# Retention attention and a two-layer MLP on one core: the first layer's weights move from GpSimd's casting DMAs into the token queue as fp32, with a cast on ScalarE

## The chip, the cores and the metric

The kernel runs on one core of a Trainium2 chip. The metric is the device time of one execution in microseconds, as the median of several runs; lower is better. In the rows of the profile PE is TensorE's matmuls, PEld its weight loads, DVE is VectorE, ACT is ScalarE, POOL is GpSimd and SP is SyncE, which here only issues DMAs.

## The reference, cut to what matters

```python
# q, k, v: fp32 [B=8, H=8, S=576, D=64]; w_in: fp32 [512, 2048]; w_out: fp32 [2048, 512]
scores = (q @ k.T) / sqrt(64)                     # per batch and head
gamma  = 1 - 2 ** (-5 - head)
Dmat   = where(i >= j, gamma ** (i - j), 0)       # causal decay
ret    = (scores * Dmat) @ v
x      = ret.transpose(0, 2, 1, 3).reshape(4608, 512)   # 4608 tokens
h      = x @ w_in                                 # first layer
g      = h * cos(h)
out    = g @ w_out                                # second layer, fp32 [4608, 512]
```

## The kernel before

**Attention.** Each sequence of 576 tokens is worked on in chunks of 64 with a running state. The kernel goes through *sessions*: the first eight take 128 tokens each (the methods `big_s` and `big`), the later ones two chunks of 64 from two streams. A session needs a tile of k and one of v (128 tokens by 512 columns, 256 KB as fp32) and a part of a tile of q (256 tokens, 512 KB), numbered in the order of use: k0, v0, q0 and so on, a new q for every second of the first sessions. SP loads them as fp32 into staging buffers: five slots `stg` for k and v, three `qstg` for q. ACT, DVE or POOL cast them to bf16 (`cast_k`, `cast_q`, `cast_v`; q and v are multiplied with decay weights as they are cast). TensorE transposes k and q (`step_tk`, `step_tq`) into PSUM, and DVE or ACT copy the result to `kt` and `qt` (`turn`). Then come the scores (`big_s`, L603), the mask by DVE (`pt`, L608), and one group of matmuls for the old state, the new state and the output (`big`, L624 to L633). The output goes to `xt`, the state to `sbd` (L584). From session 14 on the transposes are DMAs.

**First layer.** `mlp1` works on units of one PSUM bank: 512 columns, as 256 tokens by two blocks of 128 hidden features, 512 tokens by one, or 128 tokens by four. TensorE makes the unit (L711), ACT takes the cosine as a sine with a bias of pi/2 (L719), DVE multiplies (L722) into `gt`, of which there are two buffers, for even and for odd blocks of 512 tokens. There are six PSUM banks for all of this, one of them kept for filler matmuls at first. A unit needs the weights `win` of its features: `w_in` is cut into eight parts of 256 columns, w0 to w7, each for two blocks of features.

**Second layer.** For the first block of tokens `mlp2` (L736) multiplies directly; for the others `strassen` and `product` (L828) use sums of weights (`tw`, from `weight_sums`) and of tokens (`s5`, `s1`, from `token_sums`). ACT or DVE empty the banks to `os`, and SP stores.

**Order.** `schedule` adds all operations in a written order, with the pairs that may be mixed passed to `run`. A planner (`Prog.arrange`) then plays them through with assumed costs and, within a small window on each engine, takes the first that is ready in its own reckoning; in gaps of the first 24 us on TensorE it puts filler matmuls (L695). What comes out is a fixed order for each engine, with semaphore waits. Each engine works strictly in that order, and so does the queue of DMAs that SP issues.

**Weights.** `load_win` and `load_wout` are issued by POOL and cast in the DMA: fp32 in HBM, bf16 in SBUF. The five loads of `w_in` and the order with the tokens are set by these lines:

```python
WI = ((0, 1, 0), (1, 1, 0), (2, 2, 0), (4, 2, 2), (6, 2, 3))     # first part, parts, gate
GT = 1
load_to(need[0])                                                 # tokens of sessions 0 to 3
for x, n, t in WI:
    self.load_win(x, n, [("stg", t, 1, 0)] if t >= 0 else [])    # gate: v of slot t has landed
load_to(G1 + need[0], [("win", GT)])                             # next four sessions: wait for w1
```

The four loads of `w_out` (512 rows each) wait for the v tile in slot 0 (v5 at that time), and the tokens after k7 and v7 wait for the first part of `w_out`.

Of the kernel before, what the change touches and what calls it, by code (L numbers as in the profile page):

```python
# [8 lines left out]
F32 = mybir.dt.float32  # L9
# [3 lines left out]
DM, DFF = H * D, 2048  # L13
# [5 lines left out]
TB = 512  # L19
NTB = TOK // TB  # L20
NB = 6
AT = (9, 11, 12, 15)
GT = 1
C1 = ('pool', ('dve', 'pool'), 'pool')
EO, ES, EQ = ('dve', 'dve'), ('act', 'dve'), ('dve', 'dve')
WI = ((0, 1, 0), (1, 1, 0), (2, 2, 0), (4, 2, 2), (6, 2, 3))
G1, G2, WG = 4, 5, ("stg", 0, 1, 0)
FILL, SLOW = 24.0, 5.6
NF = DFF // 128
HF, HB = NF // 2, TB // 2  # L30
# [206 lines left out]
SOLO = 8  # L237


def sessions():  # L240
    out = [((uv, n), (uv, n + 1)) for uv in range(2) for n in range(0, SOLO, 2)] + [((0, SOLO),)]
    return out + [((0, n), (1, n - 1)) for n in range(SOLO + 1, NC)] + [((1, NC - 1),)]


SES = sessions()
NS = len(SES)

# [13 lines left out]
def place(uv, n):  # L261
    return SOLO * 64 * uv + 64 * n if n < SOLO else 256 * (n // 2) + 128 * uv + 64 * (n % 2)
# [14 lines left out]
def new_in(g, of):  # L277
    was = {of(*x)[0] for y in SES[:g] for x in y}
    return [x for x in dict.fromkeys(of(*x)[0] for x in SES[g]) if x not in was]


def ap(t, size, p0, n, off, *dims):
    return bass.AP(t, p0 * size + off, [[size, n]] + [list(d) for d in dims])


class Kernel:
    def __init__(self, nc, es, q, k, v, w_in, w_out, out):
# [17 lines left out]
        self.SBD = [sb(f"sbd{i}", [128, 1024], BF16) for i in range(self.NSB)]  # L305
        self.GT = [sb(f"gt{i}", [128, NF * TB], BF16) for i in range(2)]
        self.S5 = sb("s5", [128, HF * TB], BF16)
# [104 lines left out]
                bass.AP(self.src[0], (at // S * H * S + at % S) * D, [[2 * D, n], [S * D, H], [1, 2 * D]])),  # L412
                r=list(gate), w=[("qstg", slot, p0)], sem=f"q{slot}_{p0}", cost=0.62, ring=0.2 + 1.7 * n / 128, pkt=0.03)

    def load_win(self, s, n, gate=()):
        self.P.add("pool", lambda e: e.dma_start(
            ap(self.WIN, 4 * DFF, 0, 128, s * 256, [DFF, 4], [1, n * 256]),
            bass.AP(self.w_in, s * 256, [[DFF, 128], [128 * DFF, 4], [1, n * 256]])),
            r=list(gate), w=[("win", x) for x in range(s, s + n)], sem=f"wi{s}", cost=0.78, ring=1.35 * n, pkt=0.04 * n)

    def load_wout(self, s, gate=()):
        self.P.add("pool", lambda e: e.dma_start(
# [276 lines left out]
    def mlp1(self, lo, hi, fs):  # L699
# [3 lines left out]
        self.n_cb += 1  # L703
        cb, gt = self.CB[ci], self.GT[j % 2]
        xts = self.slots(lo, hi)
# [22 lines left out]
    def mlp2(self, j, t, fs, cols=(0, DM)):  # L728
        if fs[0] == 0:
            self.m2 = Box()  # L730
        box = self.m2
        gt, c0, cn = self.GT[j % 2], cols[0], cols[1] - cols[0]

# [47 lines left out]
    def token_sums(self, j, u):  # L781
        gt, f = self.GT[j % 2], 2 * u

# [19 lines left out]
    def product(self, j, m, box, t, at, first=True):  # L803
        gt = (self.GT[j % 2], NF * TB)
        wo, tw = (self.WOUT, NF * DM, DM), (self.TW, 3 * HF * HB, HB)
# [127 lines left out]
    def schedule(self):  # L933
        def req(x):
            return 1 + max(g for g in range(NS) if min(place(*y) for y in SES[g]) < x)

        need = [req(TB * (j + 1)) for j in range(NTB)]
        tiles, quads = ([new_in(g, of) for g in range(NS)] for of in (tile_of, quad_of))
        BYPE, LEAD = 14, 2
        at = {"load": 0, "cast": 0}  # L940

        def load_to(g, gate=()):
            while at["load"] < min(g, NS):
                x = at["load"]
                for t in tiles[x]:
                    self.load_kv(t, 0, gate)
                for k in quads[x]:
                    self.load_q(k, gate)
                for t in tiles[x]:
                    self.load_kv(t, 1, gate)  # L950
                at["load"] += 1

        def cast_to(g, k="pool", q=("pool", "pool"), v="pool"):
            while at["cast"] < min(g, NS):
                x = at["cast"]
                assert x < at["load"]
                for t in tiles[x]:
                    self.cast_k(t, k)
                for y in quads[x]:
                    self.cast_q(y, q)  # L960
                for t in tiles[x]:
                    self.cast_v(t, v)
                at["cast"] += 1

        def T(g):
            if g >= NS:
                return
            if g < BYPE:
                for k in quads[g]:
                    self.step_tq(k, "dve")  # L970
                for t in tiles[g]:
                    self.step_tk(t, "act")
            x = g + LEAD
            if BYPE <= x < NS:
                for k in quads[x]:
                    self.move_q(k)
                for t in tiles[x]:
                    self.move_k(t)
            load_to(g + LEAD + 4)
            cast_to(min(g + LEAD + 2, need[1]), *C1)  # L980
            cast_to(g + LEAD + 2)

        def run(mlp, att):
            n, m, k = len(att), len(mlp), 0
            for i, u in enumerate(mlp):
                u()
                while k < n * (i + 1) // m:
                    att[k]()
                    k += 1

        def att_of(g0, g1):
            out = []
            for g in range(g0, g1):
                if BIG[g] or BIG[g - 1]:
                    out.append(lambda g=g: self.step_s(g))
                out += [lambda g=g: T(g + 1), lambda g=g: self.step(g, not BIG[min(g + 1, NS - 1)]), lambda g=g: self.ev_st(g)]
            return out

        def m1(lo, hi, *fs):
            return lambda: self.mlp1(lo, hi, fs)  # L1000
# [1 line left out]
        def m2(j, t, qd):  # L1002
            return lambda: self.mlp2(j, t, range(4 * qd, 4 * qd + 4))

        load_to(need[0])
        for g in range(need[0]):
            cast_to(g + 1, "act", EQ, "dve" if g == 1 else "pool")
            for t in tiles[g]:
# [3 lines left out]
            self.step_s(g)  # L1012
            self.step(g, False, EO)
            self.ev_st(g, ES)
        for x, n, t in WI:
            self.load_win(x, n, [("stg", t, 1, 0)] if t >= 0 else [])
        load_to(G1 + need[0], [("win", GT)])
        for x in range(4):
            self.load_wout(x, [WG])
        load_to(G2 + need[0], [("wout", 0)])  # L1020
        cast_to(need[0] + 2, *C1)
        for f in range(0, 8, 2):
            self.mlp1(0, 256, (f, f + 1))
        for f in range(0, 8, 2):
            self.mlp1(256, 512, (f, f + 1))
        run([m1(0, 512, f) for f in range(8, 16)], [lambda: T(need[0])] + att_of(need[0], req(640)))
        fs = [f for u in range(HF) for f in (u, u + HF)]
        sums = [x for y in zip(self.weight_sums(0), self.weight_sums(1)) for x in y]
        fours = [range(f, f + 4) for f in range(0, 16, 4)]
# [7 lines left out]
        for j in range(1, NTB):  # L1037
# [3 lines left out]
            for i, f in enumerate(fs[:0 if last else None]):  # L1041
# [4 lines left out]
                mlp += two[i:i + 1]  # L1046
                if i in AT:
                    mlp.append(lambda u=AT.index(i), j=j: self.token_sums(j + 1, u))
            run(mlp, att_of(need[j + 1], need[j + 2]) if j + 2 < NTB else [])
# [38 lines left out]
```

## Time and profile before

| | |
|---|---|
| median of 5 runs | 306.03 us (305.66 to 307.46) |
| the profiled execution | 306.02 us, of which the profile's span is 303.0 us |
| mean granted TensorE clock | 0.989 |
| busy in the span | PE 292.5 us (97%), DVE 236.9 (78%), ACT 189.7 (63%), POOL 139.6 (46%) |
| share of the chain that ended last | PE 85%, DMA 5%, DVE 4%, SP's queue 3% |
| read from HBM, written | 36.70 MB, 9.44 MB |

The span begins with the first instruction of the program and ends with the last; the 3.0 us beside it are the start and the end of the execution. A row of a group has the line, engine, operation, what it writes and reads with the shapes and the count, then busy microseconds and the mean of one in nanoseconds, then the idle time of the engine before it and what ended that. In the chain and the timeline the first number is the start in the span and the second the length. Busy TensorE time contains the fillers. The share of the DMA engines can be above 1[...].

### The profile page before, as it was taken

How to read it: one execution, taken by the hardware profiler on the slowest of the kernel's cores; microseconds unless marked ns; L12 is line 12 of the kernel's file. 1: busy time of each engine (PE TensorE's matmuls, PEld its weight loads, DVE VectorE, ACT ScalarE, POOL GpSimd, SP SyncE). 2: the span in 40 equal slices, each digit the busy share in tenths (PEclk: the TensorE clock that was granted, in tenths of full speed). 3: DMA queues.
4: the chain of work that ended last, by engine and by line, in shares of the span. 5: the costliest groups of instructions: out<-in, count | busy, mean ns of one | idle time of the engine just before them, and what ended most of it. 6: DMA issues, size and time to landing. Idle time of an engine off the chain costs nothing.

```text
span 303.0 us, 8687 instructions
## 1 busy us (share of the span) xinstructions
PE 292.5 (97%) x3619; PEld 203.9 (67%) x3619; DVE 236.9 (78%) x382; ACT 189.7 (63%) x328; POOL 139.6 (46%) x138
## 2 busy tenths in 40 slices
PE   8984999999999999999999999999999999999996
PEld 3553658586598887666766666666667667666685
DVE  6875598998988659799958995998798668848941
ACT  5253588695698556776587658867676676546421
POOL 1426451688945289368706960993050014003213
PEclk9997799999999999999999999999999999999999
DMA  8999999999999999999899996999412010211114
GB/s 186 217 207 226 239 184 208 188 201 254 208 219 222 175 225 223 203 210 226 176 171 216 208 186 99 265 197 172 89 37 72 2 50 23 69 37 35 37 35 138
DMA packets 130629, 48.00 MB, mean 158 GB/s; under 512 B 98848, under 2 KB 130080, under 8 KB 130592
## 3 DMA queue, kind: packets, MB, share of 16 engines
q1 hardware_dynamic: 125840, 43.27, 73.8%
q0 software_dynamic: 4752, 4.19, 8.8%
q8 instruction: 28, 0.46, 0.7%
q14 instruction: 9, 0.07, 0.1%
HBM read 36.70 MB, written 9.44 MB: 152 GB/s over the span
## 4 chain that ended last, share of the span: by engine, by line
PE 85%; DMA 5%; DVE 4%; SPq 3%; ACT 1%; POOL 1%; issue 0%; DVEq 0%
PE bk L711 40%; PE bk L828 33%; DMA stg<-in_v_dram 5%; PE bk L736 3%; SPq L399 3%; PE st L550 2%; PE bk L529 2%; PE bk L520 1%; PE bk L539 1%; DVE s L794 1%; PE bk L469 1%; DVE gt L722 1%; DVE s L790 1%; PE bk L481 1%; ACT cb L719 1%; SPq L410 1%
## 5 line engine op out<-in xcount | busy, mean ns | idle before, releaser
L711 PE MATMUL bk<-xt,win 128*128 128x512 bf16 (+2 forms) x800 | 143.1, 322 | 2.0 <-DMA win<-in_moe_w_in_dram 0.9
L719 ACT ACTIVATE cb<-bk,cpi 128x512 bf16<-128x512 f32 x144 | 98.3, 688 | 59.2 <-PE bk L711 58.3
L722 DVE TENSOR_TENSOR gt<-bk,cb 128x512 bf16<-128x512 f32 x144 | 97.5, 686 | 40.0 <-ACT cb L719 34.5
L711 PEld LDWEIGHTS bk<-xt,win 128*128 128x128 bf16 x800 | 71.6, 99 | 38.9 <-DVE xt L584 1.3
L863 POOL TENSOR_TENSOR sv<-sv,os 128x512 f32<-128x512 f32 x16 | 22.9, 1431 | 78.3 <-DVE s L790 62.7
L442 POOL TENSOR_TENSOR nat<-stg,wt 128x512 bf16<-128x512 f32 x35 | 41.6, 1188 | 28.1 <-DMA stg<-in_v_dram 28.1
L584 ACT ACTIVATE sbd<-st 64x512 bf16<-64x512 f32 (+1 forms) x68 | 39.2, 577 | 14.6 <-PE bk L520 8.4
L452 POOL TENSOR_TENSOR qnat<-qstg,wt 128x512 bf16<-128x512 f32 x30 | 34.2, 1156 | 8.8 <-DMA qstg<-in_q_dram 8.7
L828 PE MATMUL bk<-tw,gt 128*128 128x256 bf16 x256 | 32.4, 273 | 0.0
L828 PE MATMUL bk<-wout,gt 128*128 128x256 bf16 x256 | 31.6, 273 | 0.7 <-DVE gt L722 0.7
L433 POOL CAST nat<-stg 128x512 bf16<-128x512 f32 x32 | 24.4, 763 | 16.4 <-DMA stg<-in_k_dram 16.4
L828 PE MATMUL bk<-wout,s 128*128 128x256 bf16 x256 | 31.7, 273 | 0.0
L828 PEld LDWEIGHTS bk<-wout,gt 128*128 128x128 bf16 x256 | 24.2, 98 | 8.7 <-DVE gt L722 3.2
L797 DVE TENSOR_TENSOR gt<-gt 128x1024 bf16<-128x1024 bf16 x32 | 30.0, 939 | 0.0
L828 PEld LDWEIGHTS bk<-tw,gt 128*128 128x128 bf16 x256 | 24.6, 98 | 7.4 <-ACT sv L867 0.6
L828 PEld LDWEIGHTS bk<-wout,s 128*128 128x128 bf16 x256 | 24.3, 98 | 7.0 <-issue 0.8
L790 DVE TENSOR_TENSOR s<-gt 128x1024 bf16<-128x1024 bf16 x32 | 27.0, 861 | 2.6 <-PE bk L828 2.5
L584 ACT ACTIVATE xt<-bk 128x256 bf16<-128x256 f32 (+1 forms) x60 | 24.4, 471 | 2.0 <-DVE pt L565 1.5
L565 DVE TENSOR_TENSOR pt<-bk,tri 128x512 bf16<-128x512 f32 (+3 forms) x35 | 20.2, 590 | 2.5 <-PE bk L520 2.5
L863 POOL TENSOR_TENSOR sv<-sv 128x512 f32<-128x512 f32 x8 | 10.7, 1336 | 23.0 <-ACT sv L867 18.7
L794 DVE TENSOR_TENSOR s<-gt 128x512 bf16<-128x512 bf16 x32 | 20.2, 640 | 0.0
L863 DVE TENSOR_TENSOR os<-bk,sv 128x512 f32<-128x512 f32 (+1 forms) x17 | 10.9, 649 | 7.4 <-POOL sv L863 6.6
(68 smaller groups left out, 261.3 us busy)
## 6 DMA issues: line engine op xcount, KB each, us to landing
stg<-in_k_dram SPq DMA_DIRECT2D x32, 256.0 KB, 4.5
stg<-in_v_dram SPq DMA_DIRECT2D x32, 256.0 KB, 5.7
out_dram<-os SPq DMA_DIRECT2D x31, 256.0 KB, 3.5
qstg<-in_q_dram SPq DMA_DIRECT2D x12, 512.0 KB, 5.9
wout<-in_moe_w_out_dram POOLq DMA_DIRECT2D x4, 512.0 KB, 11.4
win<-in_moe_w_in_dram POOLq DMA_DIRECT2D x3, 512.0 KB, 8.6
qstg<-in_q_dram SPq DMA_DIRECT2D x4, 384.0 KB, 6.2
stg<-in_k_dram SPq DMA_DIRECT2D x8, 128.0 KB, 5.7
```

Source lines behind the costliest of these rows:

```text
L433: self.P.add(eng, lambda e: e.tensor_copy(dst, src), r=r, w=w, cost=cost, port=eng == "pool")
L442: self.P.add(eng, lambda e: e.tensor_tensor(ap(self.NAT[na], 2 * DM, 0, 128, DM, [D, H], [1, D]), ap(self.STG[st], 2 * DM, 0, 128, DM, [D, ...
L452: self.P.add(eng, lambda e, x=x: e.tensor_tensor(ap(self.QNAT[slot], 2 * DM, 0, 128, x * DM, [D, H], [1, D]), ap(self.QSTG[slot], 2 * DM, ...
L584: self.P.add(eng, (lambda e: e.activation(*io(), AF.Copy)) if eng == "act" else (lambda e: e.tensor_copy(*io())), r=r, w=w, cost=0.127 + 0 ...
L711: inst = e.matmul(self.bk(box.i, 0, 128, i * n, n), ap(self.WIN, 4 * DFF, 0, 128, c * DFF + 128 * f, [1, 128]), ap(self.XT, 4 * XR, 0, 128 ...
L719: self.P.add("act", lambda e: e.activation(ap(cb, TB, 0, 128, 0, [1, m]), self.bk(box.i, 0, 128, 0, m), AF.Sin, bias=self.CPI.ap(), scale= ...
L722: self.P.add("dve", lambda e: e.tensor_tensor(ap(gt, NF * TB, 0, 128, f0 * TB + lo - TB * j, [TB, len(fs)], [1, n]), self.half_bank(box.i, ...
L790: self.P.add("dve", lambda e: e.tensor_tensor(ap(self.S5, HF * TB, 0, 128, f * TB, [1, 2 * TB]), ap(gt, NF * TB, 0, 128, f * TB, [1, 2 * TB]),
L794: self.P.add("dve", lambda e: e.tensor_tensor(ap(self.S1, HF * HB, 0, 128, f * HB, [HB, 2], [1, HB]), half(0, 0), half(1, 1), ALU.add), r= ...
L797: self.P.add("dve", lambda e: e.tensor_tensor(ap(gt, NF * TB, 0, 128, f * TB + HB, [HF * TB - HB, 2], [TB, 2], [1, HB]), ap(gt, NF * TB, 0 ...
L828: inst = e.matmul(self.bk(box.i, 0, 128, at * HB, HB), ap(lt, lsize, 0, 128, loff + f * lstep + 128 * t, [1, 128]), ap(rt, rsize, 0, 128, ...
L863: self.P.add(eng, lambda e: e.tensor_tensor(out(), a(), b(), op), r=r, w=w, cost=1.04 if eng == "pool" else 0.09 + 0.00104 * n * HB, port= ...
```

## The change

The eight parts of `w_in` are loaded by SP as fp32, at fixed places among the token loads (`WP` has, for each part, before which item of the list k0, q0, v0, k1, v1, k2, q1, v2, k3, v3, k4, q2, ... it is issued). They are staged in buffers that are first used in later stages: parts 0 to 3 in the second `gt` buffer, 4 and 5 in `s5`, 6 and 7 in `tw`. Then they are cast to `win`, part 1 by DVE and the others by ACT. The gate of the tokens on the second part is gone. In the written order the transposed q of the sessions after the first four is copied by ACT and the transposed k by DVE, the other way round than before. One number of `AT`, which says after which units the sums of tokens are added, goes from 12 to 13. `UNITS` and `EARLY` write the same units of the first layer in another form. The planner's order follows from the new costs.

```diff
@@ -19,12 +19,14 @@
 TB = 512
 NTB = TOK // TB
 NB = 6
-AT = (9, 11, 12, 15)
-GT = 1
+AT = (9, 11, 13, 15)
 C1 = ('pool', ('dve', 'pool'), 'pool')
 EO, ES, EQ = ('dve', 'dve'), ('act', 'dve'), ('dve', 'dve')
-WI = ((0, 1, 0), (1, 1, 0), (2, 2, 0), (4, 2, 2), (6, 2, 3))
+WP = (6, 8, 10, 11, 11, 12, 14, 14)
+WC = ("act", "dve", "act", "act", "act", "act", "act", "act")
 G1, G2, WG = 4, 5, ("stg", 0, 1, 0)
+EARLY = 8
+UNITS = ((0, 256, (0, 8)), (256, 512, (0, 8)), (0, 512, (8, 16)))
 FILL, SLOW = 24.0, 5.6
 NF = DFF // 128
 HF, HB = NF // 2, TB // 2
@@ -237,6 +239,11 @@
 SOLO = 8
 
 
+def ORDER(self, ts, qs):
+    k, v = ([lambda t=t, i=i: self.load_kv(t, i) for t in ts] for i in range(2))
+    return k + [lambda k=k: self.load_q(k) for k in qs] + v
+
+
 def sessions():
     out = [((uv, n), (uv, n + 1)) for uv in range(2) for n in range(0, SOLO, 2)] + [((0, SOLO),)]
     return out + [((0, n), (1, n - 1)) for n in range(SOLO + 1, NC)] + [((1, NC - 1),)]
@@ -412,11 +419,24 @@
                 bass.AP(self.src[0], (at // S * H * S + at % S) * D, [[2 * D, n], [S * D, H], [1, 2 * D]])),
                 r=list(gate), w=[("qstg", slot, p0)], sem=f"q{slot}_{p0}", cost=0.62, ring=0.2 + 1.7 * n / 128, pkt=0.03)
 
-    def load_win(self, s, n, gate=()):
-        self.P.add("pool", lambda e: e.dma_start(
-            ap(self.WIN, 4 * DFF, 0, 128, s * 256, [DFF, 4], [1, n * 256]),
-            bass.AP(self.w_in, s * 256, [[DFF, 128], [128 * DFF, 4], [1, n * 256]])),
-            r=list(gate), w=[("win", x) for x in range(s, s + n)], sem=f"wi{s}", cost=0.78, ring=1.35 * n, pkt=0.04 * n)
+    def staged(self, s):
+        if s < 4:
+            return (self.GT[1], NF * TB, s), [("gt", 1, f, x) for f in range(4 * s, 4 * s + 4) for x in range(8)]
+        if s < 6:
+            return (self.S5, HF * TB, s - 4), [("s5", f) for f in range(4 * s - 16, 4 * s - 12)]
+        return (self.TW, 3 * HF * HB, s - 6), [("tw", s - 6, x) for x in range(2)]
+
+    def load_win(self, s):
+        (t, size, i), keys = self.staged(s)
+        self.P.add("sp", lambda e: e.dma_start(
+            ap(t, size, 0, 128, 2048 * i, [512, 4], [1, 512]).bitcast(F32),
+            bass.AP(self.w_in, s * 256, [[DFF, 128], [128 * DFF, 4], [1, 256]])),
+            w=keys, sem=f"wi{s}", cost=0.62, ring=1.45, pkt=0.04)
+
+    def cast_win(self, s, eng):
+        (t, size, i), keys = self.staged(s)
+        self.copy(eng, ap(self.WIN, 4 * DFF, 0, 128, s * 256, [DFF, 4], [1, 256]),
+                  ap(t, size, 0, 128, 2048 * i, [512, 4], [1, 512]).bitcast(F32), keys, [("win", s)], 1024, True)
 
     def load_wout(self, s, gate=()):
         self.P.add("pool", lambda e: e.dma_start(
@@ -967,9 +987,9 @@
                 return
             if g < BYPE:
                 for k in quads[g]:
-                    self.step_tq(k, "dve")
+                    self.step_tq(k, "act")
                 for t in tiles[g]:
-                    self.step_tk(t, "act")
+                    self.step_tk(t, "dve")
             x = g + LEAD
             if BYPE <= x < NS:
                 for k in quads[x]:
@@ -1002,7 +1022,19 @@
         def m2(j, t, qd):
             return lambda: self.mlp2(j, t, range(4 * qd, 4 * qd + 4))
 
-        load_to(need[0])
+        items = [z for x in range(need[0] + G1) for z in
+                 ORDER(self, tiles[x], quads[x])]
+        n0 = sum(2 * len(tiles[x]) + len(quads[x]) for x in range(need[0]))
+
+        def begin(lo, hi):
+            for i in range(lo, hi):
+                for s in range(8):
+                    if WP[s] == i:
+                        self.load_win(s)
+                items[i]()
+
+        begin(0, n0)
+        at["load"] = need[0] + G1
         for g in range(need[0]):
             cast_to(g + 1, "act", EQ, "dve" if g == 1 else "pool")
             for t in tiles[g]:
@@ -1012,18 +1044,17 @@
             self.step_s(g)
             self.step(g, False, EO)
             self.ev_st(g, ES)
-        for x, n, t in WI:
-            self.load_win(x, n, [("stg", t, 1, 0)] if t >= 0 else [])
-        load_to(G1 + need[0], [("win", GT)])
+        begin(n0, len(items))
+        for x in range(8):
+            self.cast_win(x, WC[x])
         for x in range(4):
             self.load_wout(x, [WG])
         load_to(G2 + need[0], [("wout", 0)])
         cast_to(need[0] + 2, *C1)
-        for f in range(0, 8, 2):
-            self.mlp1(0, 256, (f, f + 1))
-        for f in range(0, 8, 2):
-            self.mlp1(256, 512, (f, f + 1))
-        run([m1(0, 512, f) for f in range(8, 16)], [lambda: T(need[0])] + att_of(need[0], req(640)))
+        units = [(lo, hi, range(f, f + 512 // (hi - lo))) for lo, hi, fs in UNITS for f in range(*fs, 512 // (hi - lo))]
+        for lo, hi, fs in units[:EARLY]:
+            self.mlp1(lo, hi, fs)
+        run([m1(lo, hi, *fs) for lo, hi, fs in units[EARLY:]], [lambda: T(need[0])] + att_of(need[0], req(640)))
         fs = [f for u in range(HF) for f in (u, u + HF)]
         sums = [x for y in zip(self.weight_sums(0), self.weight_sums(1)) for x in y]
         fours = [range(f, f + 4) for f in range(0, 16, 4)]
```

## The prediction

> **What bounds the kernel now.** I read four views: the page's slices, the stretches, the chain of waits in order of time, and the DMA queues.
>
> ```profile
> PE   8984999999999999999999999999999999999996
> PEclk9997799999999999999999999999999999999999
> DMA  8999999999999999999899996999412010211114
> ```
>
> Each digit is 7.6 us. From the seventh slice on TensorE is full up to the last one, so what can still move lies in the first six. There PE has its holes, and the granted clock falls to 7 tenths in the fourth and fifth slice, though the DMA row is full. Cut by hand:
>
> ```profile
> 24.20:27.77 3.57, 0.01 (x2) 0.01 (x1) 1.91 (x4) 0.40 (x1) 2.41 (x3) 0.83 1.06 262
> 27.77:36.00 8.23, 7.40 (x59) 5.53 (x60) 3.66 (x6) 3.48 (x6) 3.84 (x5) 0.66 1.17 226
> 43.00:55.00 12.00, 11.72 (x211) 10.11 (x206) 10.32 (x17) 10.54 (x18) 1.89 (x3) 1.00 1.23 202
> ```
>
> (Stretch, length, busy PE, weight load, DVE, ACT, POOL, clock, DMA, GB/s.) TensorE stands still for 3.56 us before 27.77, then works 8 us at a clock of 0.66. From 43 us on it is full, with DVE and ACT close behind. Why it stands still:
>
> ```profile
> 10.49 14.72 DMA stg<-in_v_dram
> 25.29 1.03 POOL nat L442
> 26.32 0.76 POOL win L416
> 27.09 0.63 POOL nat L433
> 27.77 0.61 PE bk L469 x4
> 29.62 0.74 DVE xt L584
> 30.41 6.83 PE bk L711 x40
> ```
>
> The fourth V tile (v3, issued at 10.49) lands at 25.21, 14.7 us later. Behind it come POOL's scaling, POOL's issue of the last w_in part (0.76), the cast of k4, the transpose, attention 3, its eviction to XT, and only at 30.41 the matmuls on tokens 256 to 511. A like load issued at 4.00 landed at 9.73. What is in its way:
>
> ```profile
> q1 hardware_dynamic: 16795, 5.10, 76.7%
> q0 software_dynamic: 2640, 2.10, 42.9%
> ```
>
> From 2 to 34 us the w_in packets (q0, POOL's queue) take 42.9% of 16 engines x 32 us: 13.7 us of all sixteen. They run beside the tokens' 256 and 512 byte packets (q1) and hold them up: k3, issued at 9.36, took 11.5 us.
>
> **The change part by part.** *Removed*: five POOL loads of w_in (4.1 us of POOL issue, 0.76 of it on the chain) and 13.7 us of engine time; and the gate by which SP waits for the second w_in part before it issues k4 (SP idle 12.83 to 18.08).
>
> *Added*: eight SP loads of 512 KB in packets of 1 KB, 4096 packets. Only the stores of the tail show such packets on q1:
>
> ```profile
> q1 hardware_dynamic: 2272, 2.10, 12.7%
> ```
>
> That is 226 to 280 us: 12.7% x 16 x 54 us / 2272 = 48 ns for 924 bytes on average. So 4096 x 48 / 16 = 12.4 us, or 1.55 us a part, against 13.7: about even. Bounds for the packet: 20 ns (a token packet at saturation: 6.5 us x 16 / 5306) and 96 ns (a q0 packet that writes 1 KB, about 1.5 MB of w_in on top of the rest: 42.9% x 512 us / 2640 gives 83 ns on average). I take 48, the same queue and size.
>
> *Moved*: the order of landings. SP's queue is served in its order; k/v tiles land 1.2 us apart, q tiles 1.9. From k2 at 10.8 (as before): w0 12.4, q1 14.3, v2 15.5, w1 17.0, k3 18.2, **v3 19.4** (before 25.2), w2 21.0, k4 22.1, w3 23.7, w4 25.2, q2 27.1, w5 28.7, v4 29.9, k5 31.0, w6 32.6, w7 34.1, v5 35.3. By the engine-time balance (12.4 against 13.7) v5 lands at 33.2 instead of 34.5; by the steps at 35.3. I take 34.5, no change: the w_out loads wait for v5 on POOL, and k8 and later wait for w_out's first part.
>
> Here a rule of the Trainium skill weighs against the change: "DMA: Bandwidth & Descriptors", Issuing engines are not separate DMA queues, says that loads of all queues run on the same 16 engines and interleave, so that another issuer saves only issue time. By the rule alone the sum is 0.76 us (POOL's issue). The rows agree on the last landing, but the row of v3 says that who interleaves decides which tile is late: 5.8 us for v3. I follow the row. The same page, Bandwidth, wants 1 MiB a transfer and gives about 2.0 us + bytes/436 GB/s for each; as an estimate eight parts of 512 KB would cost 25.6 us in series, 13 more than mine. The trace disagrees for queued loads: 256 KB land every 1.2 us, not 2.6.
>
> *Casts*: seven on ACT, one on DVE (the second part), 1024 elements. ACT's 128x512 cast takes 0.63, and 64x256 to 64x512 evictions (0.377, 0.581) give 0.8 ns an element: 1.04 us each, 7.3 in all. Bounds 0.63 and 1.26 (twice the row). DVE: between 0.42 (a 512 copy) and 1.2 (twice POOL's cast); I take 0.65, near the 0.68 of a 128x1024 copy. Each sits in order on its engine, so all that follows it waits for the landing. Also q's transposes are evicted by ACT (about 1.0 for DVE's 0.68) and k's by DVE (0.42 for ACT's 0.60): over six q and ten k about even, and 0.3 us later for a q. The staging buffers cost no wait: the second GT buffer is first needed for tokens 512 on (about 40), TW by the first weight sum (about 49), and the last cast ends at 35.7. The moved token sum (12 to 13) lies under full PE: nothing, or half a microsecond either way. SP's eight more issues (0.4 to 0.6 each where the queue has room, some 4 us) fit into the 5.2 us that its gate leaves free; POOL, five issues poorer, reaches k4 as soon as it lands.
>
> **The stage again, in the new order.**
>
> ```profile
> L719 ACT ACTIVATE cb<-bk,cpi 128x512 bf16<-128x512 f32 x24 | 16.5, 686 | 9.2 <-PE bk L711 9.2
> L722 DVE TENSOR_TENSOR gt<-bk,cb 128x512 bf16<-128x512 f32 x24 | 16.4, 688 | 5.5 <-ACT cb L719 5.1
> L608 DVE TENSOR_TENSOR pt<-bk,tr 128x512 bf16<-128x512 f32 x16 | 10.4, 683 | 1.3 <-PE bk L603 1.3
> L430 ACT ACTIVATE nat<-stg 128x512 bf16<-128x512 f32 x4 | 2.5, 630 | 6.4 <-DMA stg<-in_k_dram 6.4
> ```
>
> Up to 16.2 nothing moves. Then DVE: q1's eviction to 17.65, the w_in cast to 18.3, one product (0.69), mask 2 (1.29) to 20.3, k3's copy, a product, attention 2's evictions (0.73 + 0.43) to 22.6, mask 3 to 23.9. Attention 3 runs at 24.0 to 24.9 (before 28.1 to 29.6), its XT is there at 25.7, and the matmuls on tokens 256 to 511 start at 25.9 instead of 30.4, warm, as no PE hole before is over 1 us. Now ACT sets the pace: from 26.5 the cosines of these four units and of the first two of w4/w5 (0.69 each, 4.1 to 4.2), the w5 cast, q2's eviction to 33.6, the casts of w6 and w7 to 35.7, then cosines 3 to 5 and 39.0 for XT of attention 4, with PE held by its banks at 33.5 to 35.4 and again at 36 to 38. So XT of attention 4 comes at 39.2 against 43.29 before: 4.1. These matmuls start 4.5 us earlier, and 40 of 256 columns took 6.83 in the cold clock where 40 later ones (the chain at 60.95) took 4.37: 2.4 more, 6.9 in all, of which ACT takes 2.8 back. What follows up to the second layer (10.5 us before) has one mask pair less on DVE: 0.2 more, 4.3 in all.
>
> Does it last? The second layer would start at 49.9 (before 54.92). w_out parts land at 41.6, 45.6, 49.0 and 52.7, unchanged; in the new order two more products stand ahead of the first use of the fourth (about 54.8): no wait. DVE's first weight sum now stands ahead of k7's copy and mask and waits for the third part: DVE gets there at about 48.7, so 0.3, under these products. The tightest later row is the fifth q pair:
>
> ```profile
> 62.77 2.70 POOL L452 TENSOR_TENSOR qnat<-qstg,wt 128x512 bf16<-128x512 f32 x2 [1.42 <-DMA qstg<-in_q_dram]
> 68.78 0.61 PE L481 MATMUL bk<-idn,qnat 128*128 128x128 bf16 x8
> ```
>
> It is ready at 65.5 and used at 68.8: 3.3 us of slack, as its loads are tied to w_out's landing. The new order has 1.9 us more work ahead of it, so up to 5.2 us pass. From 75 us on the tiles run further ahead. So 4.3 us last. The profiled execution took 306.02 us (span 303.0, 3.0 around it), the median of the five is 306.03, so no correction: 306.0 - 4.3 = **301.7**.
>
> **The rivals.** *Given back later* (0.20): if v5 and so w_out land 0.8 us late and the 1.9 us do not help, the q row lets 2.5 pass: 303.5; between 302.8 and 305. For it: POOL and DMA are near full from 60 to 85. Against: the order, as it stands. *ACT less of a bound* (0.08): dense PE after 25.9 would bring XT of attention 4 at 37: 299.5. *It does not do what it says* (0.05): v3 comes early but w3 or q2 so late that the same wait returns: 305.1 to 306.9. *Slower* (0.12): the price of a 1 KB packet. At 96 ns a part takes 3.07 us, v5 and with it w_out and k8 on come 8 x 1.52 = 12.2 later, PE makes good 5.2 at most: 313. It decides from 48 + 5.2 x 16 / 4.096 = 68 ns on. For it: q0's row and the page's formula; against: the tail's row on q1 itself.
>
> **How the numbers follow.** The forecast, 2.8 to 6 us faster (300.0 to 303.2), has 0.55. 0.3% is 0.9 us, about what a measurement of this kernel can tell from no change. Faster: 0.55 + 0.20 + 0.08, less 0.03 for ends near the bound: 0.80; same 0.06; slower 0.14. The range 299.1 to 305.0 holds the forecast, nearly all of the first rival and of the dense one.
>
> **What would show it.** Right: v3 to landing about 9 us from issue; no PE hole over 1 us before 36; clock near 1.0 in the fourth and fifth slice; w_in casts of about 1.04 us on ACT; the second layer's first matmul near 50. Wrong: part loads further than 2 us apart, a w_out landing later than 43, ACT waiting for a w_in part over 1 us, or a PE wait over 2 us for q at 60 to 70.

## The result, and the profile after

The changed kernel takes 303.20 us (median of 43 runs, 301.19 to 305.26) where the kernel before takes 305.51 (80 runs, 302.40 to 308.06). The ratio is 0.9936, with a 95% interval of 0.9922 to 0.9949: 2.0 us faster by the ratio and 2.3 by the medians, where 4.3 had been forecast. Measured twice more it took 303.53 and 303.65 us (12 runs each). Beside the first of these one run of the kernel before took only 300.18, and that comparison then leaves out most of its other runs, so below kernels of the same rounds are compared by their medians.

The profiled execution took 302.65 us with a span of 300.9, against 306.02 and 303.0. The slices of its page:

```profile
PE   7988899999999999999999999999999999999996
PEclk9999999999999999999999999999999999999999
DMA  8999999999999999999999999997712020211114
```

Before the last slice PE has none under 7 any more, and the clock is granted in full throughout. The same stretches as before, where the columns are stretch, length, busy PE, weight load, DVE, ACT, POOL, clock, DMA and GB/s:

```profile
24.20:27.77 3.57, 2.76 (x38) 2.37 (x35) 2.38 (x5) 3.38 (x6) 0.41 (x1) 1.00 1.17 307
27.77:36.00 8.23, 7.15 (x65) 4.60 (x64) 6.57 (x12) 7.21 (x10) 2.79 (x3) 1.00 1.03 243
43.00:55.00 12.00, 12.00 (x172) 8.74 (x170) 9.46 (x16) 8.30 (x13) 2.35 (x3) 1.00 1.22 207
```

In the first of them TensorE works for 2.76 us where it worked for 0.01; in the second it works at a clock of 1.00 instead of 0.66. ACT is full in the first (3.38 of 3.57) and 88% busy in the second. The chain of waits in this stage (start, length, what):

```profile
14.26 7.25 DMA gt<-in_moe_w_in_dram
...
21.52 1.06 ACT win L450
...
22.64 1.06 PE bk L731 x8
...
24.41 0.94 ACT win L450
```

Up to 26 us no token load is on it: what TensorE waits for now is the third and fourth w_in part and their casts (0.99 us at 22.64, 0.81 at 25.41). v3 lands at 19.88 instead of 25.21, the matmuls on tokens 256 to 511 start at 25.41 instead of 30.41, XT of attention 4 is evicted at 39.25 instead of 43.29, and the second layer starts at 49.91 instead of 54.92. In this profile the forecast of the stage was right to a few tenths. A second profile of the same kernel (e5 below) was less lucky: tokens 256 to 511 at 26.02, XT of attention 4 at 39.86, the second layer at 51.34.

But this lead does not last. I count the matmul columns that are left at each moment, and compare at which time each kernel has as many left: TensorE is 4.8 us ahead at 55 us and still 4.8 at 105, then 4.4 at 115, 3.9 at 130, 3.3 at 150, 2.65 at 190, and 2.16 from 205 to the end. (In e5's profile it is 3.4 at 55, 3.5 at 105 and 1.2 from 205 on: 1.4 less of a lead, and nearly the same loss.) TensorE's waits between 110 and 205 us say who takes it (what waited, for whom: us in all, how many, the longest):

```profile
PE bk L848 <- DVE gt L742: 1.8, 3, 0.7
PE bk L549 <- issue: 0.4, 1, 0.4
PE bk L731 <- ACT xt L604: 0.3, 1, 0.3
```

The same view of the kernel before is empty. The three long waits (0.56, 0.71 and 0.50 us at 140, 170 and 201) are those of a new token block's first Strassen product (L848) for one of the block's last products of the gate on VectorE (L742). "issue" means that the profile names no releaser; that wait ended just after a product on VectorE (117.20 us) too. VectorE's row of instructions ahead of the second:

```profile
167.24 1.52 DVE L810 TENSOR_TENSOR s<-gt 128x1024 bf16<-128x1024 bf16 x1
168.69 0.68 DVE L742 TENSOR_TENSOR gt<-bk,cb 128x512 bf16<-128x512 f32 x1
169.29 0.67 DVE L883 TENSOR_TENSOR os<-bk,sv 128x512 f32<-128x512 f32 x1
169.88 0.68 DVE L742 TENSOR_TENSOR gt<-bk,cb 128x512 bf16<-128x512 f32 x1
```

VectorE doesn't idle there; it is late. A token sum of 0.67 us (as at 109.42) takes 1.52 while GpSimd prepares tokens. That alone is not new: the 32 such sums took 0.86 us in the mean before the change and 0.88 after it. VectorE was also as full before, when TensorE did not wait for it. The same stretch of the kernel before and of the changed one (busy VectorE is 31.93 and 30.37 us):

```profile
110.00:145.00 35.00, 35.00 (x528) 24.80 (x525) 31.93 (x45) 25.11 (x46) 25.96 (x24) 1.00 1.16 216
110.00:145.00 35.00, 33.78 (x456) 22.59 (x455) 30.37 (x45) 22.96 (x42) 23.04 (x23) 1.00 1.09 215
```

The DMA share is above 1 in both, with no other queue than SP's carrying data.

### The profile page after: what moved, and what is told of

It is laid out like the page before. It is cut to its first block, busy times and chain, and to the rows that moved or that the text cites. A ratio compares the mean times of both kernels' runs of the same rounds, so it can differ in the third digit from the quotient of the medians.

```text
span 300.9 us, 8677 instructions
## 1 busy us (share of the span) xinstructions
PE 289.5 (96%) x3618; PEld 202.5 (67%) x3618; DVE 234.9 (78%) x388; ACT 195.7 (65%) x331; POOL 137.4 (46%) x133
## 2 busy tenths in 40 slices
DMA packets 132213, 50.09 MB, mean 166 GB/s; under 512 B 98896, under 2 KB 131664, under 8 KB 132176
## 4 chain that ended last, share of the span: by engine, by line
PE 68%; DMA 11%; DVE 8%; SPq 6%; issue 3%; ACT 2%; POOL 2%; DVEq 0%
PE bk L848 30%; PE bk L731 29%; DMA wout<-in_moe_w_out_dram 4%; SPq L406 3%; DVE gt L742 3%; DMA gt<-in_moe_w_in_dram 2%; PE bk L756 2%; SPq L431 2%; DMA stg<-in_v_dram 2%; DMA qstg<-in_q_dram 2%; PE st L570 2%; PE bk L549 2%; DVE os L883 1%; PE bk L540 1%; PE bk L559 1%
## 5 line engine op out<-in xcount | busy, mean ns | idle before, releaser
L731 PE MATMUL bk<-xt,win 128*128 128x512 bf16 (+2 forms) x800 | 141.4, 320 | 3.1 <-ACT win L450 1.8
L742 DVE TENSOR_TENSOR gt<-bk,cb 128x512 bf16<-128x512 f32 x144 | 96.8, 686 | 38.7 <-ACT cb L739 34.0
L883 POOL TENSOR_TENSOR sv<-sv,os 128x512 f32<-128x512 f32 x16 | 22.1, 1384 | 75.6 <-DVE s L810 50.0
L604 ACT ACTIVATE sbd<-st 64x512 bf16<-64x512 f32 (+1 forms) x68 | 39.2, 577 | 15.6 <-PE bk L540 11.5
L472 POOL TENSOR_TENSOR qnat<-qstg,wt 128x512 bf16<-128x512 f32 x30 | 35.8, 1213 | 15.9 <-DMA qstg<-in_q_dram 15.8
L848 PE MATMUL bk<-wout,gt 128*128 128x256 bf16 x256 | 31.6, 273 | 2.5 <-DVE gt L742 2.5
L848 PE MATMUL bk<-tw,gt 128*128 128x256 bf16 x256 | 32.2, 273 | 0.0
L848 PE MATMUL bk<-wout,s 128*128 128x256 bf16 x256 | 31.8, 273 | 0.0
L848 PEld LDWEIGHTS bk<-wout,gt 128*128 128x128 bf16 x256 | 24.3, 98 | 10.4 <-DVE gt L742 5.1
L848 PEld LDWEIGHTS bk<-tw,gt 128*128 128x128 bf16 x256 | 24.6, 98 | 8.0 <-ACT sv L887 1.3
L848 PEld LDWEIGHTS bk<-wout,s 128*128 128x128 bf16 x256 | 24.3, 98 | 6.3 <-issue 0.4
L585 DVE TENSOR_TENSOR pt<-bk,tri 128x512 bf16<-128x512 f32 (+2 forms) x36 | 20.3, 579 | 2.1 <-PE bk L540 2.0
L814 DVE TENSOR_TENSOR s<-gt 128x512 bf16<-128x512 bf16 x32 | 18.4, 582 | 0.0
L887 ACT ACTIVATE sv<-bk 128x512 f32<-128x512 f32 x16 | 9.6, 598 | 12.1 <-PE bk L848 12.1
```

The source lines that it names most:

```text
L472: self.P.add(eng, lambda e, x=x: e.tensor_tensor(ap(self.QNAT[slot], 2 * DM, 0, 128, x * DM, [D, H], [1, D]), ap(self.QSTG[slot], 2 * DM, ...
L585: inst = e.tensor_tensor(ap(pt, 1024, p0, n, 256 * x, [256, m], [64, 4], [1, 64]), ap(self.BK, NB * 512, p0, n, (lo, hi)[x] * 512 + 256, [ ...
L604: self.P.add(eng, (lambda e: e.activation(*io(), AF.Copy)) if eng == "act" else (lambda e: e.tensor_copy(*io())), r=r, w=w, cost=0.127 + 0 ...
L731: inst = e.matmul(self.bk(box.i, 0, 128, i * n, n), ap(self.WIN, 4 * DFF, 0, 128, c * DFF + 128 * f, [1, 128]), ap(self.XT, 4 * XR, 0, 128 ...
L742: self.P.add("dve", lambda e: e.tensor_tensor(ap(gt, NF * TB, 0, 128, f0 * TB + lo - TB * j, [TB, len(fs)], [1, n]), self.half_bank(box.i, ...
L848: inst = e.matmul(self.bk(box.i, 0, 128, at * HB, HB), ap(lt, lsize, 0, 128, loff + f * lstep + 128 * t, [1, 128]), ap(rt, rsize, 0, 128, ...
```

## The experiments

Three theories stood at the start. The early gain could be that of the landing order, or of the queue and the fp32 form. The late loss could be VectorE's order at the ends of blocks, its whole load, or the token stream. And the swap of the transposes' evictions could matter or not. Line numbers in the experiments' profiles are shifted by the lines that an edit adds.

**Only the order of landings (e2).** The kernel before, with new gates alone:

```
-WI = ((0, 1, 0), (1, 1, 0), (2, 2, 0), (4, 2, 2), (6, 2, 3))
+WI = ((0, 1, 0), (1, 1, 2), (2, 2, 3), (4, 2, 3), (6, 2, 3))
```

> The kernel before, with w_in still loaded by GpSimd and cast on the way, but three gates changed: the second part of w_in waits for the third V tile, all later parts for the fourth (v3). So only the order of the landings is taken from the change. Theory A (the gain is that v3 no longer shares the DMA engines with w_in): v3 lands at 16 to 18.5 instead of 25.2, attention 3 runs 4 us or more sooner, and most of the early gain of 4.8 us is there; as the parts then come late (the third at about 23), 302 to 304 at the end. Rival B (it needs the other queue or the fp32 form: the parts of w_in beside the tokens are as slow as ever and now also late): tokens 0 to 255 wait for w_in, 305 to 307.

It took 306.92 us against 305.11 (ratio 1.0048, 1.0016 to 1.008). v3 landed at 18.10 and the matmuls on tokens 256 to 511 started at 25.79, as in the changed kernel; at 30 us TensorE was 4.1 us ahead of the kernel before. At 45 us 1.1 was left. The waits of TensorE from 20 to 60 us:

```profile
PE bk L711 <- DVE xt L584: 1.5, 1, 1.5
PE st L629 <- DVE pt L608: 1.1, 1, 1.1
PE bk L711 <- ACT xt L584: 0.8, 1, 0.8
PE bk L624 <- DVE pt L608: 0.4, 1, 0.4
```

v4, issued a microsecond sooner than before (20.35 instead of 21.43), lands at 34.39 here (28.78 before, 29.96 in the changed kernel), v5 at 36.74 and v6 at 40.68: six of the eight w_in parts are issued together from 19.17 on, and hold up the next tokens as they had held up v3. After the two waits near 41 us TensorE also works at half the clock for a while:

```profile
41.00:42.00 1.00, 0.26 (x11) 0.10 (x4) 1.00 (x2) 0.70 (x2) 1.00 (x3) 1.00 1.14 179
43.00:44.00 1.00, 1.00 (x12) 1.00 (x11) 1.00 (x3) 0.22 (x2) 1.00 (x1) 0.50 1.22 197
```

So the order alone makes the early gain. What keeps it in the changed kernel this run does not show, since its order is not that of the change: there w6 and w7 stand behind k5. The price of the parts is not the difference. Their packets, added up, took 13.7 us of all sixteen DMA engines before, 13.3 in e2 and 14.2 in the changed kernel (96 ns in the median for one that reads 2 KB and writes 1 KB on GpSimd's queue, 49 for one of 1 KB on SP's). Theory A was right on the early gain, rival B on the time at the end. A run with the old queue and the changed kernel's places for all eight parts is missing.

**The casts (e3).** Three casts moved from ScalarE to GpSimd:

```
-WC = ("act", "dve", "act", "act", "act", "act", "act", "act")
+WC = ("act", "dve", "act", "act", "act", "pool", "pool", "pool")
```

> The changed kernel with the last three casts of w_in (parts 5, 6, 7) on GpSimd instead of ScalarE. Theory A (ScalarE sets the pace from 26 to 39 us, as forecast): 3.2 us less on ScalarE there, XT of attention 4 at 37.5 to 38.3 instead of 39.25, the lead over the kernel before at 50 us 5.6 to 6.5 instead of 4.75; at the end 301.2 to 302.4, less or more as VectorE's later order falls. Rival B (the late landings of parts 6 and 7, at 32.7 and 35.1, and GpSimd's slower casts, about 2 us each by its 1.03 for 512 columns, set the pace just as well): XT of attention 4 at 39 to 40.5, 303 to 304.5.

Both missed: 311.65 us (6 runs), 1.0222 of the kernel before (1.0178 to 1.0266). GpSimd's cast took 1.05 us, not 2: the 1.03 us of the expectation were those of a scaling, and a cast of 512 columns takes GpSimd 0.61. The waits of TensorE from 26 to 80 us:

```profile
PE bk L623 <- DVE kt L481: 3.2, 1, 3.2
PE bk L501 <- POOL qnat L472: 1.9, 1, 1.9
PE bk L731 <- POOL win L453: 1.8, 1, 1.8
```

GpSimd waits for the seventh part to land (idle for 3.88 us up to 34.03), and TensorE for its cast. But the larger part, as far as the trace tells, is order: the scaling of q3 on GpSimd starts at 39.74, sooner than in the changed kernel (41.18), and TensorE waits for it only because the planner has now set q3's and k's transposes in front of first-layer matmuls. The clock falls as well, to 0.50 from 44 to 48 us. So this run says little of how far ScalarE sets the pace; it does show that an engine changed for three casts reorders the rest.

**One sum moved (e1).** After planning, S5 of the third pair of rows goes behind the product of row 7 (in blocks 6 to 8 it then adds rows that the difference has already overwritten):

```
+        for op in [x for x in self.ops if getattr(x, "lazy", False) and x.w[0] == ("s5", 4)]:
+            i = self.ops.index(op)
+            late = [n for n in range(i, i + 30) if self.ops[n].eng == "dve" and self.ops[n].w[0][::2] == ("gt", 7)]
+            if late:
+                self.ops.insert(late[0], self.ops.pop(i))
```

> Against the changed kernel (303.2) this moves one instruction of each token block: the token sum S5 of the third pair of rows, which stands ahead of the product of row 7 on VectorE, goes to just behind that product. Nothing else is reordered. In the trace of the changed kernel TensorE waits 0.56, 0.71 and 0.50 us at 140, 170 and 200 us for that product, which the kernel before does not. Theory A (the sum in front of the product is what the waits are made of): the three waits are gone, 1.2 to 1.8 us faster than the changed kernel, 301.4 to 302.0. Rival B (VectorE is late by its whole load there, and the next product or the sums of S5 are then what TensorE waits for): 0 to 0.4 us faster, 302.8 to 303.2, with waits of like sum at neighbouring places.

304.78 us, beside 305.11 for the kernel before (ratio 0.9985, 0.9959 to 1.0012). The waits of TensorE from 110 to 205 us:

```profile
PE bk L736 <- ACT xt L609: 1.1, 2, 0.8
PE bk L554 <- DVE pt L590: 0.8, 1, 0.8
```

The three waits are gone, and 1.9 us of others have come: for a mask (L590) and for an XT whose mask came late, each behind a moved sum. That is rival B, by the trace. Against the changed kernel the time can't be read here, since that did not run in these rounds, and their loads landed later with the same order (last w_out part at 56.9 instead of 54.6 us).

**Half of the sums' work, and lighter stores (e5, e6, e7).** The changed kernel again as the reference; the token sums of blocks 2 to 5 on half of their elements, in the same order; and stores of a quarter of the columns. The edits of e6 and e7:

```
+        w5, w1 = (TB, HB // 2) if 2 <= j <= 5 else (2 * TB, HB)
...
-            ap(self.S5, HF * TB, 0, 128, f * TB, [1, 2 * TB]), ...
+            ap(self.S5, HF * TB, 0, 128, f * TB, [1, w5]), ...
```

```
+        cw = cn // 4 if s < 6 * TB else cn
...
-                bass.AP(self.out, row * DM + c0, [[DM, m], [1, cn]]),
+                bass.AP(self.out, row * DM + c0, [[DM, m], [1, cw]]),
```

> The changed kernel itself once more, in the same rounds as the next three, as their reference, since a like order of instructions (the sum moved) came out 1.5 us later at 60 us than the first profile of the changed kernel. Theory A: 302.7 to 303.7, as before; its PE lead over the kernel before shrinks from over 3.5 us at 105 us to about 2 at 205 again. Rival B (the first profile was a lucky one): the lead at 60 us is nearer 2.5 to 3.5 than 4.9 and the time 303.5 to 305.

> The changed kernel with the token sums of blocks 2 to 5 at half width (S5, S1 and the difference each on half of its elements; the other half keeps old values); the order of the instructions stays as it is, VectorE has some 4 us less in each 30 us from 110 us on. Theory A (TensorE leads, but VectorE's work is not ahead by as much, and from 110 to 205 TensorE gives its lead back waiting for VectorE): the waits of TensorE between 110 and 205 (2.4 us in the changed kernel) fall below 0.7, 1.7 to 2.6 us faster than the changed kernel of the same rounds. Rival B (the lead is lost to the stream of the token loads, or to ScalarE): less than 0.7 faster, waits for ACT xt or for masks in their place.

> The changed kernel with every store of the output's first 3072 rows cut to a quarter of its columns (the rest is not written): some 5 MB less for the DMA engines between 80 and 230 us, as many instructions and the same order. Theory A (VectorE is what the lead is lost to, and it is late by its own work): within 0.7 us of the changed kernel. Rival B (the DMA engines are full to 205 us, the token loads come no sooner than in the kernel before though TensorE is ahead, and so masks and products are late): k and v tiles from 100 us on land 1 us or more sooner and 1.3 to 2.6 us are gained.

The changed kernel took 303.53 us beside 305.25 for the kernel before. On the early lead rival B was right: 3.5 us at 60 us, and the first profile with its 4.9 was a lucky one; the time fits both ranges. The second and the fourth w_in part landed at 17.75 and 24.88 instead of 16.65 and 23.98. With half sums 301.50, 2.0 us less (drawing again and again from the 12 runs of each, 1.05 to 2.8; ratio 0.9933, 0.9908 to 0.9965). With light stores 303.31, the same (ratio 0.9993, 0.9972 to 1.0017). A stretch and the waits with half sums:

```profile
110.00:145.00 35.00, 34.65 (x463) 23.25 (x460) 24.96 (x44) 23.82 (x43) 21.24 (x22) 1.00 1.13 226
```

```profile
PE bk L849 <- DVE gt L742: 0.6, 1, 0.6
PE bk L731 <- ACT xt L604: 0.3, 1, 0.3
```

VectorE is busy for 24.96 of 35 us; in the changed kernel it was 30.37. TensorE's waits are 0.9 instead of 2.5 us, and its lead over the kernel before is 3.9 us at 210 instead of 2.16. The lead shrinks by 1.0 us after 105 us, where it shrank by 2.6 in the changed kernel's first profile and by 2.3 in its second. This is theory A, though the waits were to fall below 0.7. The stretch and the waits with light stores:

```profile
110.00:145.00 35.00, 33.61 (x455) 22.43 (x453) 31.49 (x45) 22.70 (x42) 25.79 (x23) 1.00 0.97 181
```

```profile
PE bk L848 <- DVE gt L742: 1.7, 3, 0.7
PE bk L549 <- issue: 0.6, 1, 0.6
PE bk L731 <- ACT xt L604: 0.3, 1, 0.3
```

The DMA share falls from 1.09 to 0.97, and the 25th k load lands at 118.2 instead of 122.2 us; TensorE waits as long as in the changed kernel, at the same places. So from 110 us on the token stream is not what takes the lead: the amount of VectorE's work is.

**Relief for VectorE without leaving work out (e8, e11, e12).** S1 on GpSimd (e8):

```
-        self.P.add("dve", lambda e: e.tensor_tensor(
+        self.P.add("pool", lambda e: e.tensor_tensor(
             ap(self.S1, HF * HB, 0, 128, f * HB, [HB, 2], [1, HB]), half(0, 0), half(1, 1), ALU.add),
-            r=keys(0, 0) + keys(1, 1), w=[("s1", f), ("s1", f + 1)], cost=0.36, port=True, lazy=True)
+            r=keys(0, 0) + keys(1, 1), w=[("s1", f), ("s1", f + 1)], cost=1.2, port=True, lazy=True)
```

Then the sums of the third pair behind the block's last products, in the changed kernel (e11) and in e8's (e12):

```
+        for what, to in ((("s5", 4), ("gt", 15)), (("s1", 4), ("s5", 6)), (("gt", 4), ("s5", 6))):
+            for op in [op for op in self.ops if getattr(op, "lazy", False) and key(op) == what]:
+                i = self.ops.index(op)
+                for n in [n for n in range(i, min(i + 80, len(self.ops))) if key(self.ops[n]) == to][:1]:
+                    self.ops.insert(n, self.ops.pop(i))
```

> The changed kernel with the four S1 sums of every token block (128x512, bf16, 0.41 us on VectorE) on GpSimd, which is busy for 46% of the span; the planner lays the rest anew. Theory A (VectorE's work is what limits from 110 to 205): VectorE is 1.6 us lighter in each 30 us, half of the waits go, 1 to 1.8 us faster than the changed kernel of the same rounds, if GpSimd's sums (1.2 us each) don't hold the tokens' scaling. Rival B (the two share what they read through: VectorE's 1024-element sums already take 1.3 to 1.5 instead of 0.67 where GpSimd works): no gain or up to 1.5 us slower.

> The changed kernel as it is, in the same rounds as the next three, as their reference. By both of its earlier measurements: 302.9 to 303.9; waits of TensorE between 110 and 205 us of 2 to 2.6 us in all, most of them for the last products of a token block.

> The changed kernel with VectorE's sums of the third pair of rows taken from in front of the last products of each token block: S5 goes behind the product of row 15, S1 and the difference behind the next S5; all else stays in order. Theory A (VectorE is short of time just before the end of a block, not over the block as a whole): the last products come 1.3 to 2.4 us sooner, the waits for them fall from 1.5 to under 0.5 us, 1 to 2 us faster than the changed kernel, 301.3 to 302.5. Rival B (VectorE is short over the whole block, as when one S5 alone was moved): waits for S5, masks or XT take their place, within 0.7 us.

> The same move in the kernel with the S1 sums on GpSimd, where TensorE's waits for the last products were 0.98 and 0.97 us at 170 and 200 us and nothing else of size remained. Theory A: these two go and nothing takes their place since VectorE has 1.6 us less in each block, 1.2 to 2 us faster than the changed kernel, 301.3 to 302.3, the best of all. Rival B (GpSimd's S1 sums, or S5 now late, become what TensorE waits for): 303 to 304.5.

With S1 on GpSimd (e8) it took 303.20 us beside 303.53, no difference (ratio 0.9989, 0.9967 to 1.0039). TensorE's waits from 110 to 205:

```profile
PE bk L848 <- DVE gt L742: 1.9, 2, 1.0
PE bk L731 <- ACT xt L604: 0.3, 1, 0.3
```

The changed kernel beside the last two took 303.65 (kernel before 305.83; ratio 0.9902, 0.9863 to 0.9941). e11 took 305.65 and e12 307.04, 2.0 and 3.4 us more (ratios 1.0066, 1.0013 to 1.0141, and 1.0111, 1.0064 to 1.0184). The waits of e11 from 80 to 205 us, the largest:

```profile
PE bk L559 <- issue: 2.7, 2, 2.1
PE bk L559 <- DVE gt L752: 1.1, 1, 1.1
PE bk L741 <- ACT xt L614: 0.9, 2, 0.5
```

The first Strassen product no longer waits for the block's last products, and larger waits of the attention (L559 reads its queries and states) stand in their place. The longest of them, which the profile gives to nobody, ends at 120.60, just after a product on VectorE that ends at 120.50; e12 shows 2.4 us of waits for XT. So the mechanism of rival B was right in both, VectorE is short over the whole block, and an order that helps one user takes from another; but both times lie beyond rival B's ranges, on the slow side.

In e8 its own rival B was right, that VectorE and GpSimd get in each other's way. VectorE's sums that stayed got longer: the sum S5 took 0.97 us instead of 0.90 in e5, the difference 1.18 instead of 0.94 (means of 32). About half of the 20.5 us of S1 sums came back in this way. This fits a rule of the Trainium skill ("SBUF — State Buffer", Who interferes with whom): a VectorE instruction with two inputs in SBUF contends with a GpSimd instruction that reads SBUF. The changed kernel's trace shows it on the sums, which read two SBUF tensors (0.68 us where GpSimd stood still, up to 1.78 where it worked), and not on the products, which read one PSUM bank and one SBUF tensor (0.69 and 0.68).

**The swap of the evictions undone (e4, e10).** The changed kernel, once without and once with its own reference:

```
-                    self.step_tq(k, "act")
+                    self.step_tq(k, "dve")
...
-                    self.step_tk(t, "dve")
+                    self.step_tk(t, "act")
```

> The changed kernel with one part of the change undone: the transposes of q are evicted by VectorE again and those of k by ScalarE. Theory A (that swap is about even, as forecast, and the late loss is that of the planner's order): early lead within 0.5 us of 4.75 at 50 us, 302.7 to 303.7 at the end. Rival B (the swap is what makes VectorE late from 110 us on): the waits at 140, 170 and 200 us are gone, 301 to 302.

> The changed kernel with the transposes of q evicted by VectorE again and those of k by ScalarE, beside the changed kernel in the same rounds. Theory A (the swap carries a part of the gain: it takes the 1.0 us evictions of q off the engine that the lead is later lost on, and the order that follows is better): 1.2 to 3.2 us slower than the changed kernel. Rival B (about even, as forecast; the earlier 306.4 came from later landings in those rounds): within 0.9 us.

Undone, it took 306.44 us in the first rounds (ratio to the kernel before 1.0061, 1.0023 to 1.0098), above both ranges of e4; 305.71 beside 303.65 in the second, 2.06 us slower than the changed kernel (0.63 to 4.4; ratio 1.0068, 1.0021 to 1.0144), as theory A of e10 had it. The waits of TensorE in e4 from 40 to 110 us:

```profile
PE bk L623 <- DVE gt L742: 0.9, 1, 0.9
PE bk L731 <- ACT xt L604: 0.5, 1, 0.5
PE bk L731 <- ACT kt L480: 0.3, 1, 0.3
PE bk L756 <- DMA wout<-in_moe_w_out_dram: 0.2, 1, 0.2
PE bk L489 <- POOL nat L453: 0.2, 1, 0.2
```

The changed kernel has 0.2 us of waits in this stretch. So the swap carries about as much as the whole net gain, within that wide interval. It does not cause the late loss: the waits for last products are there without it as well (1.9 us between 110 and 210). How much is the engine of the eviction, and how much the order that the planner then lays, was not separated.

## Why the prediction was right or wrong

**The number.** 303.20 us lies in the range and at the very edge of the forecast (300.0 to 303.2), and it lies there partly by luck. The early part came as forecast in one profile and 0.9 us short in the other; the loss after 105 us, 2.3 to 2.6 us, was put at nothing; and about 0.9 us of the gain came from outside the span, where the sum had nothing.

**Landings and the price of a packet: right for v3, w_out missed.** v3 landed at 19.88 (forecast 19.4), q2 at 27.29 (27.1), w7 at 35.07 (34.1). The slower rival, with 96 ns a packet, was far off. But the 48 ns were too few as well: the tail's average held 224 packets of 4 bytes, and its packets of 1 KB alone took 52.5 ns in the mean. Those of w_in took 55.5 (53.4 in e5), so the eight parts cost 14.2 us of all engines instead of 12.4. v5, taken at 34.5, landed at 35.92, beyond the bound of 35.3, and w_out, "unchanged", at 44.1, 47.5, 50.9 and 54.6: 2 us late. The fourth part came just in time for its use, forecast for about 54.8. Two of the signs of being wrong did appear: w_out later than 43, and ACT waiting 1.53 us for the third w_in part. The formula for one transfer, which the prediction sets aside, stands in the Trainium skill ("DMA: Bandwidth & Descriptors") under Anatomy of one DMA, SWDGE (gpsimd) path: it was fitted to loads that GpSimd issues, not to SP's.

**Casts and the stage: right in the first profile.** 1.06 us a cast on ACT (1.04), 0.68 on DVE (0.65). Tokens 256 to 511 at 25.41 (25.9), XT of attention 4 at 39.25 (39.2), the second layer at 49.91 (49.9). The cold clock went with the hole before it, as the step on the clock had it; that holes up to 1 us are harmless does not hold in general, since in e2 two of 1.13 and 0.84 us, the ends 1.4 us apart, were followed by it. What was not seen: TensorE is held there by w_in's own casts (1.8 us in both profiles), not by the XT of attention 3.

**The rule on issuing engines.** By the rule alone the sum was 0.76 us, by the row of v3 far more. e2 bears out the row: with the same issuer and another order v3 landed at 18.10, so the order gives the early gain and not the issuer. But it bears out a part of the rule too: what is moved from before v3 stands before v4.

**"So 4.3 us last": the step that failed.** The last wait that I followed was that of the fifth q pair. It came at 63.07 and cost nothing, so the mechanism of the rival "given back later" was not the one at work, though its 303.5 is near the result. I followed only TensorE and its loads past 75 us, as if every engine were 4.3 us ahead. In the trace TensorE is, and the others are not: GpSimd's 5th to 29th preparations of a k or v tile, from 30 to 89 us, start between 0.3 us sooner and 1.9 us later than before (the 5th at 30.03 instead of 29.01, the 13th at 60.40 instead of 58.96, the 29th at 88.72 instead of 87.48), because most tokens from k5 on land 1 to 2 us later up to 60 us. VectorE has their masks still to do when TensorE already asks for the next block's products, and from 110 to 145 it has little room: 31.93 of 35 us busy in the kernel before, without a wait of TensorE, because TensorE came later, as I read it. e6 shows that less work on VectorE keeps 1.6 of the 2.6 us that are lost; e7 that sooner tokens from 100 us on keep none. That the later tokens of 40 to 90 us are where VectorE's arrears begin is argued from the trace and was not tried.

**The swap "about even": wrong.** Its own durations were right (1.02 us for q on ACT, 0.42 for k on DVE, by the groups), but a step was costed by its engine time where it also changes the order of everything planned after it. Undoing it cost about 2 us (0.6 to 4.4).

**The time around the span: missed.** I carried the 3.0 us of the profiled execution over. The changed kernel has 1.74 (median of 44, 1.69 to 1.89), and the kernel before has 2.56 to 2.71 in the later rounds (1.91 to 3.27 in single runs). So of the profiled 3.37 us, 2.1 are span and 1.27 lie around it; by the medians in the rounds of e5 and e9 1.0 to 1.2 and 0.9. In the terms of my sum: 4.8 instead of 4.3 early, 2.6 given back, 1.27 from a place that the sum did not have. In the terms of the second profile: 3.5 early, 2.3 given back.

**What stays open.** Every kernel with an early lead lost some of it from 110 to 205 us. How much of the net gain is only the clock is open too. In the rounds of e1, e5 and e9 the kernel before took 305.9 us in the median of its 61 runs with a mean clock of 0.989 and 304.5 in 33 with 0.994; its two runs with 1.0 throughout took 302.66 and 300.18 (span 298.2), no more than the changed kernel's 303.6 (24 runs of e5 and e9). So the kernel before may be as fast where its clock does not fall, and its order may keep a lead that the new order loses; there is no trace of such a run. No version here beats the changed kernel; e6 is faster only by leaving sums out.

## What to carry to other kernels

When an early stage gets faster, ask for each engine and each stream whether it gets ahead as well; a lead that TensorE alone has is slack taken from the others, and it is handed back where the next engine is nearly full, even 60 us later. A load moved out of one tile's way stands in the way of another, so list what lands later, not only what lands sooner. In a planned kernel a change of engine is also a change of order: measure it alone before calling it even.

## What I had not expected of the hardware

- The time around the span moved with the change: 2.6 to 2.7 us before, 1.74 after, 2.0 with the old loads behind new gates (e2), 1.5 with three casts on GpSimd (e3). No trace shows what lies there.
- The granted clock was 0.989 or 0.994 as a mean in nearly all later runs of the kernel before and 1.0 or 0.999 in all of the changed kernel's 24. In the profiles the low clock follows idle time of TensorE: one stretch of 3.56 us in the kernel before, two of 1.13 and 0.84 us close together in e2; two of 0.99 and 0.81 us in the changed kernel, their ends 2.8 us apart, left it at 1.00.
- One cast of 128x1024 took 1.06 us on ACT, 1.05 on GpSimd and 0.68 on DVE, so GpSimd was no slower than ACT.
- Some 4.7 MB less to store (45.37 instead of 50.09 MB moved) did not change the time (between 0.9 us less and 0.5 more), though the DMA row had read full up to 205 us.
